# Loading the FFN weights by casting DMAs, V straight into its padded tile, and the first two batches by head pairs, in a fused ReLU²-attention and SwiGLU kernel

## The chip, the cores and the metric

The kernel runs on one core of one Trainium2 chip. The metric is device time in microseconds (us) of one execution. The engines are called PE (TensorE, matmuls), PEld (its weight loads), DVE (VectorE), ACT (ScalarE), POOL (GpSimd) and SP (SyncE, which here only issues DMAs).

## The reference

```python
def _attn_ref(q, k, v):                      # each (8, 12, 448, 64), float32
    scores = (1 / sqrt(64)) * (q @ k.T)
    attn = np.maximum(scores, 0.0) ** 2 / 448
    return attn @ v

def _moe_ref(x, w_gate, w_val, w_out, rms_g):   # x: (3584, 768)
    xn = x / sqrt(mean(x * x) + 1e-6) * rms_g
    g = xn @ w_gate                          # (768, 1536)
    val = xn @ w_val                         # (768, 1536)
    return (g * sigmoid(g) * val) @ w_out    # (1536, 768)

# x is the attention's output, (8, 12, 448, 64) -> (8*448, 12*64)
```

Each of the three weight matrices has 768 x 1536 float32 values, 4.72 MB. The output is float32.

## The kernel before

The kernel computes in bf16. It handles one batch of attention as six head pairs (2 x 64 = 128 partitions). While it computes the attention of batch b it inserts the FFN of batch b-1 in chunks ("fillers") between and inside the pairs. Batch 0 has no FFN to insert. There the fillers are 60 pieces of weight loading, ten per pair: a float32 piece comes by a DMA on SP's queue into one of four staging tiles, and ScalarE casts it into the bf16 weight tile.

```python
wstage = ctx.enter_context(tc.tile_pool(name="wstage", bufs=4))
ldpool = ctx.enter_context(tc.tile_pool(name="ld", bufs=2))
apool  = ctx.enter_context(tc.tile_pool(name="attn", bufs=10))
# ... cut ...
def _wload(src_d, dst_sb, kt, o, w):                 # 60 of these: wwork
    st = wstage.tile([P, WCH], FP32, name="wst", tag="wst")
    nc.sync.dma_start(out=st[:, :w], in_=src_d[:, kt, o : o + w])
    nc.scalar.copy(out=dst_sb[:, kt, o : o + w], in_=st[:, :w])
# ... cut ...
def load_batch(b):
    if b == 0:      # per pair and per tensor: tiles qp, kp, vp by casting GpSimd DMAs
        ...
    # other batches: one casting GpSimd DMA each for q, k and v: tiles qb, kb, vb
# ... cut ...
def attention_pair(b, j, xT, qkv, fillers=()):
    # PE transposes q and k into psT; ScalarE copies them to QT and KT
    # ... cut ...
    vpad = ldpool.tile([PC, NCH, 2, P], BF16, name="vpad", tag="vpad")
    nc.vector.tensor_copy(out=vpad[:, :, 0, 0:D], in_=vb[:, :, 0, :])
    nc.vector.tensor_copy(out=vpad[:, :, 0, D:P], in_=zero_bf[:PC])
    nc.vector.tensor_copy(out=vpad[:, :, 1, 0:D], in_=zero_bf[:PC])
    nc.vector.tensor_copy(out=vpad[:, :, 1, D:P], in_=vb[:, :, 1, :])
    for c in range(NCH):
        # PE: psS = K Q^T for both heads; ScalarE: ReLU of the first (rA);
        # VectorE: ReLU of the second (rB), and both squares
        ...
    if fillers: fillers.pop(0)()
    # PE: psAV += vpad^T rA / rB, eight matmuls
    if fillers: fillers.pop(0)()
    nc.scalar.mul(out=xT[:, j, :], in_=psAV[:], mul=inv_attn)
    for f in fillers: f()
# ... cut ...
# main loop: the fillers are the FFN chunks of batch b-1, and wwork for b == 0
```

A scheduler fixes the order of instructions on each engine when the kernel is built.

Of the kernel before, what the change touches and what calls it, by code (L numbers as in the profile page):

```python
# [9 lines left out]
FP32 = mybir.dt.float32  # L10
BF16 = mybir.dt.bfloat16
# [7 lines left out]
def kernel(  # L19
# [11 lines left out]
    nc = tc.nc  # L31
    P = nc.NUM_PARTITIONS

    B, H, S, D = q.shape
    T, DM = out.shape
    DMw, F = moe_w_gate.shape
# [3 lines left out]
    NCH = 4  # L40
    assert S % NCH == 0
    PC = S // NCH
    assert PC <= P
    assert DM % P == 0 and F % P == 0
    KT = DM // P
    FT = F // P
    HP = H // 2
# [12 lines left out]

    const_pool = ctx.enter_context(tc.tile_pool(name="consts", bufs=1))
    wpool = ctx.enter_context(tc.tile_pool(name="weights", bufs=1))
    wstage = ctx.enter_context(tc.tile_pool(name="wstage", bufs=4))
    ldpool = ctx.enter_context(tc.tile_pool(name="ld", bufs=2))
    tpool = ctx.enter_context(tc.tile_pool(name="tsb", bufs=2))
    apool = ctx.enter_context(tc.tile_pool(name="attn", bufs=10))
    xpool = ctx.enter_context(tc.tile_pool(name="xT", bufs=2))
    npool = ctx.enter_context(tc.tile_pool(name="norm", bufs=2))
    hpool = ctx.enter_context(tc.tile_pool(name="hT", bufs=2))
# [18 lines left out]
    zero_bf = const_pool.tile([P, NCH, D], BF16, name="zero_bf", tag="zero_bf")  # L88
# [2 lines left out]
    g_sb = wpool.tile([P, KT], FP32, name="g_sb", tag="rmsg")  # L91
    nc.sync.dma_start(out=g_sb[:], in_=moe_rms_g.rearrange("(kt p) -> p kt", p=P))

    wg_sb = wpool.tile([P, KT, F], BF16, name="wg_sb", tag="wg")
    wv_sb = wpool.tile([P, KT, F], BF16, name="wv_sb", tag="wv")
    wo_sb = wpool.tile([P, FT, DM], BF16, name="wo_sb", tag="wo")
    wg_d = moe_w_gate.rearrange("(kt p) f -> p kt f", p=P)
    wv_d = moe_w_val.rearrange("(kt p) f -> p kt f", p=P)
    wo_d = moe_w_out.rearrange("(fk p) m -> p fk m", p=P)
    WCH = 512  # L100
    wwork: list = []

    def _wload(src_d, dst_sb, kt, o, w):
        st = wstage.tile([P, WCH], FP32, name="wst", tag="wst")
        nc.sync.dma_start(out=st[:, :w], in_=src_d[:, kt, o : o + w])
        nc.scalar.copy(out=dst_sb[:, kt, o : o + w], in_=st[:, :w])

    for src_d, dst_sb, nk in ((wg_d, wg_sb, KT), (wv_d, wv_sb, KT), (wo_d, wo_sb, FT)):
        W = dst_sb.shape[-1]
        for kt in range(nk):  # L110
            for o in range(0, W, WCH):
                w = min(WCH, W - o)
                wwork.append(
                    lambda a=(src_d, dst_sb, kt, o, w): _wload(*a)
                )

    def qkv_batch_ap(t: bass.AP, b: int) -> bass.AP:
        return t[b].rearrange("h (p c) d -> p c h d", c=NCH)

    def qkv_pair_ap(t: bass.AP, b: int, j: int) -> bass.AP:  # L120
        return t[b, 2 * j : 2 * j + 2].rearrange("h (p c) d -> p c h d", c=NCH)

    def out_rows_ap(b: int) -> bass.AP:
        return out[b * S : (b + 1) * S, :].rearrange("(p u) m -> p u m", u=NCH)

    def load_batch(b: int):
        if b == 0:
            out_tiles = []
            for j in range(HP):
                trip = []  # L130
                for src, tg in ((q, "qp"), (k, "kp"), (v, "vp")):
                    t = ldpool.tile([PC, NCH, 2, D], BF16, name=tg, tag=tg)
                    nc.gpsimd.dma_start(out=t[:], in_=qkv_pair_ap(src, b, j))
                    trip.append(t[:])
                out_tiles.append(tuple(trip))
            return out_tiles
        big = []
        for src, tg in ((q, "qb"), (k, "kb"), (v, "vb")):
            t = ldpool.tile([PC, NCH, H, D], BF16, name=tg, tag=tg)
            nc.gpsimd.dma_start(out=t[:], in_=qkv_batch_ap(src, b))  # L140
            big.append(t)
        return [
            tuple(t[:, :, 2 * j : 2 * j + 2, :] for t in big) for j in range(HP)
        ]

    def attention_pair(b: int, j: int, xT: bass.AP, qkv, fillers=()):
        fillers = list(fillers)
        qb, kb, vb = qkv
        QT = tpool.tile([P, S], BF16, name="QT", tag="QT")
        KT_ = tpool.tile([P, S], BF16, name="KT", tag="KT")  # L150
        psT = psum.tile([P, 2, S], BF16, name="psT", tag="psS", bufs=PSS_BUFS)
        for ti, (src, dst) in enumerate(((qb, QT), (kb, KT_))):
            for c in range(NCH):
                nc.tensor.transpose(  # L154
                    out=psT[:, ti, c * PC : (c + 1) * PC],
                    in_=src[:, c, :, :],
                    identity=ident[:],
                )
            nc.scalar.copy(out=dst[:], in_=psT[:, ti, :])  # L159

        vpad = ldpool.tile([PC, NCH, 2, P], BF16, name="vpad", tag="vpad")
        nc.vector.tensor_copy(out=vpad[:, :, 0, 0:D], in_=vb[:, :, 0, :])
        nc.vector.tensor_copy(out=vpad[:, :, 0, D:P], in_=zero_bf[:PC])
        nc.vector.tensor_copy(out=vpad[:, :, 1, 0:D], in_=zero_bf[:PC])
        nc.vector.tensor_copy(out=vpad[:, :, 1, D:P], in_=vb[:, :, 1, :])  # L165

        psAV = psum.tile([P, S], FP32, name="psAV", tag="psAV", bufs=1)
        rsq = [[None] * NCH, [None] * NCH]
        for c in range(NCH):
            pss = []  # L170
            for hh in range(2):
                prt = slice(hh * D, (hh + 1) * D)
                if b == 0:
                    tg, bf = _ps0_tags[(j * NCH * 2 + c * 2 + hh) % len(_ps0_tags)]
                else:
                    tg, bf = "psS", PSS_BUFS
                psS = psum.tile([PC, S], FP32, name="psS", tag=tg, bufs=bf)
                nc.tensor.matmul(  # L178
                    out=psS[:],
                    lhsT=KT_[prt, c * PC : (c + 1) * PC],  # L180
                    rhs=QT[prt, :],
                    start=True,
                    stop=True,
                )
                pss.append(psS)
            rA = apool.tile([PC, S], BF16, name="rA", tag="rA")
            nc.scalar.activation(out=rA[:], in_=pss[0][:], func=ACT.Relu)  # L187
            nc.vector.tensor_tensor(out=rA[:], in0=rA[:], in1=rA[:], op=ALU.mult)  # L188
            rsq[0][c] = rA
            rB = apool.tile([PC, S], BF16, name="rB", tag="rA")  # L190
            nc.vector.tensor_relu(out=rB[:], in_=pss[1][:])  # L191
            nc.vector.tensor_tensor(out=rB[:], in0=rB[:], in1=rB[:], op=ALU.mult)  # L192
            rsq[1][c] = rB
        if fillers:
            fillers.pop(0)()
        for hh in range(2):
            for c in range(NCH):
                nc.tensor.matmul(  # L198
                    out=psAV[:],
                    lhsT=vpad[:, c, hh, :],  # L200
                    rhs=rsq[hh][c][:],
                    start=(hh == 0 and c == 0),
                    stop=(hh == 1 and c == NCH - 1),
                )
        if fillers:
            fillers.pop(0)()
        nc.scalar.mul(out=xT[:, j, :], in_=psAV[:], mul=inv_attn)  # L207
        for f in fillers:
            f()
# [98 lines left out]
    for b in range(NB):  # L308
        xT = xpool.tile([P, KT, S], BF16, name="xT", tag="xT")
        xTs.append(xT)  # L310
        qkvs = load_batch(b)
        if b >= 1:
            work = ffn_chunks(b - 1, xTs[b - 1])
        else:
            work = wwork
        per = (len(work) + HP - 1) // HP
        wi = 0
        for j in range(HP):
            fl = work[wi : wi + per]
            wi += len(fl)  # L320
            attention_pair(b, j, xT, qkvs[j], fillers=fl)
        while wi < len(work):
            work[wi]()
            wi += 1
# [31 lines left out]
```

## Time and profile before

The median is 678.0 us (675.4 to 682.0, 16 runs). Three times of the profiled execution (span 677.0 us):

| what | time |
|---|---|
| first gate matmul (psG), where the FFN of batch 0 begins | 104.6 us |
| PE busy before it, and after it | 51.0 of 104.6 us; 537.7 of 572.4 us |
| time between the normalisations of successive batches later on (taken at their square root, tile rstdb) | 75.1 to 75.7 us |

The first fence is from the page: busy time of each engine, then three rows of the span in 40 slices of 17 us (a digit is the busy share in tenths; PEclk is the granted clock in tenths).

```profile
PE 588.8 (87%) x3120; PEld 296.7 (44%) x3120; DVE 463.2 (68%) x1088; ACT 272.5 (40%) x517; POOL 69.8 (10%) x48
PE   0655469999899989999899979999899989997997
PEclk9999999999699988999699989999799989999899
DMA  9999940069100890069001890079000110001002
```

PE is the limit from the seventh slice on. The first six slices, about 104 us, are different: PE is half idle while the DMA engines are busy. The clock row reads 9 there, but the matmuls themselves say otherwise. A score matmul (psS) took 577 ns (median, 20 to 40 us) and 393 ns later, from 180 to 220 us. The Trainium skill, "TensorE: Matmul & The Clock Gate", Part 1, says that an idle PE gets half its clock and gets the full clock after about 3.4 us of sustained work. The trace agrees with the half: near 181 us, where the clock row dips, successive gate and value matmuls start 0.37 us apart, and 0.19 us apart at 190 us. Before 108.4 us the clock column must not be read: the trace has no clock record there, its first record is a change to full speed, and the views count time without a record as full speed.

The second fence is the table of waits of the window 0 to 104 us. The columns are who waited for whom, then us in total, number of waits, longest one.

```profile
PE psT L154 <- ACT QT L159: 20.1, 7, 9.8
ACT wv_sb L106 <- DMA wst<-in_moe_w_val_dram: 14.8, 14, 2.4
ACT wg_sb L106 <- DMA wst<-in_moe_w_gate_dram: 12.9, 11, 2.7
ACT wo_sb L106 <- DMA wst<-in_moe_w_out_dram: 12.6, 12, 1.9
```

ScalarE waited 40 us (14.8 + 12.9 + 12.6) for staged weights, and PE waited 20 us for ScalarE's copy of a transposed q. The third fence, from the timeline (start, us, engine, line, instruction, count, idle time before it and what ended that):

```profile
18.19 0.62 ACT L106 CAST wg_sb<-wst 128x512 bf16<-128x512 f32 x1 [1.51 <-DMA wst<-in_moe_w_gate_dram]
18.72 0.53 ACT L159 COPY QT<-psT 128x448 bf16<-128x448 bf16 x1
19.30 0.53 PE L154 MATMUL psT<-ident,kp 112*128 112x112 bf16 x4 [9.79 <-ACT QT L159]
```

The first q had landed at 8.95 us, where its transposes start. The copy that takes them out of PSUM (the memory that PE writes to) ran at 18.72, because it stands behind casts in ScalarE's fixed order, and each cast waits for its own load. PE stood for 9.79 us. The skill's "TensorE: Matmul & The Clock Gate", Part 1, in the passage on engine queue depths, calls ScalarE's queue strictly first in, first out.

The last fence is from the view of DMA queues for 0 to 100 us (queue, kind, packets, MB, share of the 16 engines' time).

```profile
q0 software_dynamic: 48768, 6.19, 96.9%
q1 hardware_dynamic: 9424, 14.16, 49.5%
```

The staged weights (q1) moved 14.16 MB in about 100 us, while GpSimd's queue (q0: batches 0, 1 and 2 of q, k and v) held the same engines with many small packets. The packets of the two queues overlap in time, so the shares add up to more than 100%.

### The profile page before, as it was taken

Reading aid. Unit: us, or ns where it says so; the run is one execution under the profiler, and the core shown is the slowest. Engines: PE = TensorE matmul, PEld = TensorE weight load, DVE = VectorE, ACT = ScalarE, POOL = GpSimd, SP = SyncE. Lnnn points to the kernel's source line nnn. Section 1 sums busy time; section 2 is a strip of 40 time slices with the busy share of each in tenths; the row PEclk is TensorE's granted clock in tenths of the full one; section 3 lists DMA queues with packets and bytes.
Section 4 is the critical chain, followed back from the end, with each engine's and each line's share of the span. In section 5 each row is a group of like instructions: output and inputs, shape, how many; then the busy total and the mean of one; then the engine's idle time right before and its main releaser. Section 6 shows DMA issues by size and latency. Waiting matters only on the chain. (4 is left out here: it accounts for less than half of the span.)

```text
span 677.0 us, 8435 instructions
## 1 busy us (share of the span) xinstructions
PE 588.8 (87%) x3120; PEld 296.7 (44%) x3120; DVE 463.2 (68%) x1088; ACT 272.5 (40%) x517; POOL 69.8 (10%) x48
## 2 busy tenths in 40 slices
PE   0655469999899989999899979999899989997997
PEld 0212124456244544456344644455344634454455
DVE  0533369786888679775888678866978578857552
ACT  3755573532544243532534243433434253422210
POOL 5653000012001200012001200012000000000000
PEclk9999999999699988999699989999799989999899
DMA  9999940069100890069001890079000110001002
GB/s 197 219 233 225 207 125 1 1 41 135 30 0 4 89 113 1 1 41 145 20 0 12 89 105 1 1 62 143 1 1 1 42 42 0 1 21 61 1 1 81
DMA packets 143208, 42.22 MB, mean 62 GB/s; under 512 B 131904, under 2 KB 133440, under 8 KB 143168
## 3 DMA queue, kind: packets, MB, share of 16 engines
q0 software_dynamic: 129648, 16.52, 38.2%
q1 hardware_dynamic: 13520, 25.17, 12.5%
q8 instruction: 24, 0.39, 0.2%
q14 instruction: 16, 0.13, 0.1%
HBM read 47.19 MB, written 11.01 MB: 86 GB/s over the span
## 5 line engine op out<-in xcount | busy, mean ns | idle before, releaser
L256 PE MATMUL psG<-xn,wg_sb 128*128 128x448 bf16 x576 | 152.0, 365 | 6.8 <-DVE xn L238 4.4
L191 DVE TENSOR_SCALAR rB<-psS 112x448 bf16<-112x448 f32 x192 | 116.8, 616 | 45.2 <-PE psS L178 45.2
L265 PE MATMUL psV<-xn,wv_sb 128*128 128x448 bf16 x576 | 140.5, 360 | 0.2 <-DVE hT L276 0.2
L289 PE MATMUL psO<-wo_sb,hT 128*112 128x512 bf16 (+1 forms) x768 | 136.2, 327 | 0.0
L178 PE MATMUL psS<-QT,KT 64*112 64x448 bf16 x384 | 92.4, 428 | 32.7 <-ACT rA L187 14.5
L289 PEld LDWEIGHTS <-hT 128*112 128x112 bf16 x768 | 90.4, 130 | 38.5 <-issue 7.0
L187 ACT ACTIVATE rA<-psS 112x448 bf16<-112x448 f32 x192 | 97.7, 541 | 18.5 <-PE psS L178 17.8
L273 ACT ACTIVATE sig<-psG 128x448 bf16<-128x448 f32 x96 | 51.4, 543 | 115.5 <-PE psG L256 77.8
L188 DVE TENSOR_TENSOR rA<-rA 112x448 bf16<-112x448 bf16 x192 | 73.3, 382 | 23.8 <-ACT rA L187 23.3
L265 PEld LDWEIGHTS <-wv_sb 128*128 128x128 bf16 x576 | 54.7, 99 | 65.3 <-issue 22.7
L256 PEld LDWEIGHTS <-wg_sb 128*128 128x128 bf16 x576 | 55.3, 100 | 61.6 <-issue 23.5
L275 DVE TENSOR_TENSOR t<-sig,psG 128x448 bf16<-128x448 bf16 x96 | 58.6, 616 | 33.2 <-ACT sig L273 31.9
L198 PE MATMUL psAV<-rA,vpad 112*128 112x448 bf16 x192 | 66.7, 405 | 10.6 <-DVE rA L188 9.6
L192 DVE TENSOR_TENSOR rB<-rB 112x448 bf16<-112x448 bf16 x192 | 73.4, 382 | 0.1
L276 DVE TENSOR_TENSOR hT<-t,psV 128x448 bf16<-128x448 bf16 x96 | 59.3, 618 | 17.4 <-PE psV L265 13.7
L296 DVE COPY ost<-psO 112x512 f32<-112x512 f32 x64 | 35.5, 555 | 48.0 <-PE psO L289 48.0
L178 PEld LDWEIGHTS <-KT 64*112 64x112 bf16 x384 | 29.8, 140 | 87.2 <-issue 56.6
L207 ACT ACTIVATE xT<-psAV 128x448 bf16<-128x448 f32 x48 | 26.2, 546 | 98.6 <-PE psAV L198 98.6
L198 PEld LDWEIGHTS <-vpad 112*128 112x128 bf16 x384 | 38.2, 107 | 57.7 <-issue 33.8
L198 PE MATMUL psAV<-rB,vpad 112*128 112x448 bf16 x192 | 59.4, 414 | 0.0
L159 ACT COPY QT<-psT 128x448 bf16<-128x448 bf16 x48 | 25.4, 530 | 79.4 <-PE psT L154 79.4
L140 POOL DMA_DIRECT2D vb<-in_v_dram x7 | 16.6, 2372 | 290.3 <-DVE vpad L165 290.3
(41 smaller groups left out, 344.5 us busy)
## 6 DMA issues: line engine op xcount, KB each, us to landing
out_dram<-ost SPq DMA_DIRECT2D x32, 336.0 KB, 2.7
qb<-in_q_dram POOLq DMA_DIRECT2D x7, 672.0 KB, 9.3
kb<-in_k_dram POOLq DMA_DIRECT2D x7, 672.0 KB, 12.5
vb<-in_v_dram POOLq DMA_DIRECT2D x7, 672.0 KB, 8.9
wst<-in_moe_w_gate_dram SPq DMA_DIRECT2D x18, 256.0 KB, 5.0
wst<-in_moe_w_val_dram SPq DMA_DIRECT2D x18, 256.0 KB, 6.5
wst<-in_moe_w_out_dram SPq DMA_DIRECT2D x12, 256.0 KB, 6.5
wst<-in_moe_w_out_dram SPq DMA_DIRECT2D x12, 128.0 KB, 6.1
```

Of the source, the lines that this page charges most:

```text
L178: nc.tensor.matmul(out=psS[:], lhsT=KT_[prt, c * PC : (c + 1) * PC], rhs=QT[prt, :], start=True, stop=True,)
L187: nc.scalar.activation(out=rA[:], in_=pss[0][:], func=ACT.Relu)
L188: nc.vector.tensor_tensor(out=rA[:], in0=rA[:], in1=rA[:], op=ALU.mult)
L191: nc.vector.tensor_relu(out=rB[:], in_=pss[1][:])
L192: nc.vector.tensor_tensor(out=rB[:], in0=rB[:], in1=rB[:], op=ALU.mult)
L198: nc.tensor.matmul(out=psAV[:], lhsT=vpad[:, c, hh, :], rhs=rsq[hh][c][:], start=(hh == 0 and c == 0), stop=(hh == 1 and c == NCH - 1),)
L256: nc.tensor.matmul(out=psG[:], lhsT=wg_sb[:, kt, fb * P : (fb + 1) * P], rhs=xn[:, kt, :], start=(kt == 0), stop=(kt == KT - 1),)
L265: nc.tensor.matmul(out=psV[:], lhsT=wv_sb[:, kt, fb * P : (fb + 1) * P], rhs=xn[:, kt, :], start=(kt == 0), stop=(kt == KT - 1),)
L273: nc.scalar.activation(out=sig[:], in_=psG[:], func=ACT.Sigmoid)
L275: nc.vector.tensor_tensor(out=t1[:], in0=sig[:], in1=psG[:], op=ALU.mult)
L276: nc.vector.tensor_tensor(out=hT[:, fb, :], in0=t1[:], in1=psV[:], op=ALU.mult)
L289: nc.tensor.matmul(out=psO[:, :w], lhsT=hT[:, fk, u * PC : (u + 1) * PC], rhs=wo_sb[:, fk, o : o + w], start=(fk == 0), stop=(fk == FT - 1),)
```

## The change

The intent is to take the weight staging off SP and ScalarE, to take the V copies off VectorE, and to have everything that start-up needs requested early:

1. Each weight matrix comes by one GpSimd DMA that casts float32 to bf16 on the way. The staging pool, 60 loads and 60 casts go.
2. V comes by two GpSimd DMAs per pair straight into the padded tile. Of four VectorE copies per pair the two zero fills remain, given to any engine.
3. Batches 0 and 1 are loaded by pairs, with six buffers per tile in place of two. The order of requests is batch 0, wg, wv, batch 1's pairs 0 to 2, wo, batch 1's pairs 3 to 5.
4. The pool for rA and rB grows from 10 to 20 buffers.

```diff
-    wstage = ctx.enter_context(tc.tile_pool(name="wstage", bufs=4))
-    apool = ctx.enter_context(tc.tile_pool(name="attn", bufs=10))
+    apool = ctx.enter_context(tc.tile_pool(name="attn", bufs=20))
... cut ...
+    def load_vpad(b: int, j: int):
+        vpad = ldpool.tile([PC, NCH, 2, P], BF16, name="vpad", tag="vpad", bufs=6)
+        nc.any.tensor_copy(out=vpad[:, :, 0, D:P], in_=zero_bf[:PC])
+        nc.any.tensor_copy(out=vpad[:, :, 1, 0:D], in_=zero_bf[:PC])
+        nc.gpsimd.dma_start(out=vpad[:, :, 0, 0:D], in_=v_head_ap(b, 2 * j))
+        nc.gpsimd.dma_start(out=vpad[:, :, 1, D:P], in_=v_head_ap(b, 2 * j + 1))
+        return vpad
... cut: load_batch(b, pairs): q and k by pairs with bufs=6 for batches 0 and 1, whole
... batches later; V always by load_vpad; the result for batch 1 is kept in `early` ...
-    def _wload(src_d, dst_sb, kt, o, w):
-        st = wstage.tile([P, WCH], FP32, name="wst", tag="wst")
-        nc.sync.dma_start(out=st[:, :w], in_=src_d[:, kt, o : o + w])
-        nc.scalar.copy(out=dst_sb[:, kt, o : o + w], in_=st[:, :w])
... cut ...
+    def load_weights():
+        nc.gpsimd.dma_start(out=wg_sb[:], in_=moe_w_gate.rearrange("(kt p) f -> p kt f", p=P))
+        nc.gpsimd.dma_start(out=wv_sb[:], in_=moe_w_val.rearrange("(kt p) f -> p kt f", p=P))
+        first = load_batch(1, range(0, 3))
+        nc.gpsimd.dma_start(out=wo_sb[:], in_=moe_w_out.rearrange("(fk p) m -> p fk m", p=P))
+        early[1] = first + load_batch(1, range(3, HP))
... cut: the four vpad copies leave attention_pair ...
         qkvs = load_batch(b)
-        if b >= 1:
+        if b == 0:
+            load_weights()
+            work = []
+        else:
             work = ffn_chunks(b - 1, xTs[b - 1])
-        else:
-            work = wwork
```

More of the change, by code (lines that the diff above doesn't have):

```diff
@@ L92, with qk_batch_ap, qk_pair_ap, v_head_ap @@
     nc.sync.dma_start(out=g_sb[:], in_=moe_rms_g.rearrange("(kt p) -> p kt", p=P))
+    def qk_batch_ap(t: bass.AP, b: int) -> bass.AP:
+        return t[b].rearrange("h (p c) d -> p c h d", c=NCH)
+    def qk_pair_ap(t: bass.AP, b: int, j: int) -> bass.AP:
+        return t[b, 2 * j : 2 * j + 2].rearrange("h (p c) d -> p c h d", c=NCH)
+    def v_head_ap(b: int, h: int) -> bass.AP:
+        return v[b, h].rearrange("(p c) d -> p c d", c=NCH)
+    def out_rows_ap(b: int) -> bass.AP:
+        return out[b * S : (b + 1) * S, :].rearrange("(p u) m -> p u m", u=NCH)
+    def load_vpad(b: int, j: int):
[5 more added lines that the diff above has]
+        return vpad
+    early: dict = {}
+    def load_batch(b: int, pairs=None):
+        if b in early:
+            return early[b]
+        if b == 0 or pairs is not None:
+            trips = []
+            for j in pairs if pairs is not None else range(HP):
+                qkp = []
+                for src, tg in ((q, "qp"), (k, "kp")):
+                    t = ldpool.tile([PC, NCH, 2, D], BF16, name=tg, tag=tg, bufs=6)
+                    nc.gpsimd.dma_start(out=t[:], in_=qk_pair_ap(src, b, j))
+                    qkp.append(t[:])
+                trips.append((qkp[0], qkp[1], load_vpad(b, j)))
+            return trips
+        big = []
+        for src, tg in ((q, "qb"), (k, "kb")):
+            t = ldpool.tile([PC, NCH, H, D], BF16, name=tg, tag=tg)
+            nc.gpsimd.dma_start(out=t[:], in_=qk_batch_ap(src, b))
+            big.append(t)
+        return [
+            (
+                big[0][:, :, 2 * j : 2 * j + 2, :],
+                big[1][:, :, 2 * j : 2 * j + 2, :],
+                load_vpad(b, j),
+            )
+            for j in range(HP)
+        ]
     wg_sb = wpool.tile([P, KT, F], BF16, name="wg_sb", tag="wg")
@@ L96 @@
     wo_sb = wpool.tile([P, FT, DM], BF16, name="wo_sb", tag="wo")
-    wg_d = moe_w_gate.rearrange("(kt p) f -> p kt f", p=P)
-    wv_d = moe_w_val.rearrange("(kt p) f -> p kt f", p=P)
-    wo_d = moe_w_out.rearrange("(fk p) m -> p fk m", p=P)
-    WCH = 512
-    wwork: list = []
-    def _wload(src_d, dst_sb, kt, o, w):
-        st = wstage.tile([P, WCH], FP32, name="wst", tag="wst")
-        nc.sync.dma_start(out=st[:, :w], in_=src_d[:, kt, o : o + w])
-        nc.scalar.copy(out=dst_sb[:, kt, o : o + w], in_=st[:, :w])
@@ L108 @@
-    for src_d, dst_sb, nk in ((wg_d, wg_sb, KT), (wv_d, wv_sb, KT), (wo_d, wo_sb, FT)):
-        W = dst_sb.shape[-1]
-        for kt in range(nk):
-            for o in range(0, W, WCH):
-                w = min(WCH, W - o)
-                wwork.append(
-                    lambda a=(src_d, dst_sb, kt, o, w): _wload(*a)
-                )
-    def qkv_batch_ap(t: bass.AP, b: int) -> bass.AP:
-        return t[b].rearrange("h (p c) d -> p c h d", c=NCH)
-    def qkv_pair_ap(t: bass.AP, b: int, j: int) -> bass.AP:
-        return t[b, 2 * j : 2 * j + 2].rearrange("h (p c) d -> p c h d", c=NCH)
@@ L123, in out_rows_ap @@
-    def out_rows_ap(b: int) -> bass.AP:
-        return out[b * S : (b + 1) * S, :].rearrange("(p u) m -> p u m", u=NCH)
-    def load_batch(b: int):
-        if b == 0:
-            out_tiles = []
-            for j in range(HP):
-                trip = []
-                for src, tg in ((q, "qp"), (k, "kp"), (v, "vp")):
-                    t = ldpool.tile([PC, NCH, 2, D], BF16, name=tg, tag=tg)
-                    nc.gpsimd.dma_start(out=t[:], in_=qkv_pair_ap(src, b, j))
-                    trip.append(t[:])
-                out_tiles.append(tuple(trip))
-            return out_tiles
-        big = []
-        for src, tg in ((q, "qb"), (k, "kb"), (v, "vb")):
-            t = ldpool.tile([PC, NCH, H, D], BF16, name=tg, tag=tg)
-            nc.gpsimd.dma_start(out=t[:], in_=qkv_batch_ap(src, b))
-            big.append(t)
-        return [
-            tuple(t[:, :, 2 * j : 2 * j + 2, :] for t in big) for j in range(HP)
-        ]
+    def load_weights():
+        nc.gpsimd.dma_start(
+            out=wg_sb[:], in_=moe_w_gate.rearrange("(kt p) f -> p kt f", p=P)
+        )
+        nc.gpsimd.dma_start(
+            out=wv_sb[:], in_=moe_w_val.rearrange("(kt p) f -> p kt f", p=P)
+        )
+        first = load_batch(1, range(0, 3))
+        nc.gpsimd.dma_start(
+            out=wo_sb[:], in_=moe_w_out.rearrange("(fk p) m -> p fk m", p=P)
+        )
+        early[1] = first + load_batch(1, range(3, HP))
@@ L146, in attention_pair @@
     def attention_pair(b: int, j: int, xT: bass.AP, qkv, fillers=()):
         fillers = list(fillers)
-        qb, kb, vb = qkv
+        qb, kb, vpad = qkv
         QT = tpool.tile([P, S], BF16, name="QT", tag="QT")
@@ L159, in attention_pair @@
             nc.scalar.copy(out=dst[:], in_=psT[:, ti, :])
-        vpad = ldpool.tile([PC, NCH, 2, P], BF16, name="vpad", tag="vpad")
-        nc.vector.tensor_copy(out=vpad[:, :, 0, 0:D], in_=vb[:, :, 0, :])
-        nc.vector.tensor_copy(out=vpad[:, :, 0, D:P], in_=zero_bf[:PC])
-        nc.vector.tensor_copy(out=vpad[:, :, 1, 0:D], in_=zero_bf[:PC])
-        nc.vector.tensor_copy(out=vpad[:, :, 1, D:P], in_=vb[:, :, 1, :])
         psAV = psum.tile([P, S], FP32, name="psAV", tag="psAV", bufs=1)
```

## The prediction

> **What bounds the kernel now.** Two stages.
> (a) Start-up, 0 to about 104 us. By the tile view of wg_sb the first gate matmul runs at 104.6 us. The windows view gives PE 46.7 us of 100 busy up to there, while DMA moves 157 to 232 GB/s until 95 us: batch 0's and 1's q, k, v, batch 2's and all weights (14.2 MB as float32) share the engines. The timeline shows batch 0's pairs starved: first q issued at 1.6 us, landed at 8.95; loads have two buffers, so GpSimd issues later ones only when slots come free; a pair takes about 10 us. ScalarE's 60 weight casts (0.62 or 0.40 us) wait for staging loads and sit between the copies and ReLUs that PE needs. Matmuls here take 0.53-0.59 us: slow clock.
> (b) From 104 us on PE is the limit: 28 matmuls per 5 us, PE busy 95-100%, period 75.1-75.7 us per batch (GpSimd's q issues at 156.6, 232.3, 308.0, 383.7, 458.8). Exception: at each batch boundary the normalisation leaves about 4 us of PE gaps, and the granted clock falls to 0.50-0.65 for some 10 us. The Trainium skill, "TensorE: Matmul & The Clock Gate", Part 1, says an idle PE drops to half rate until it has been busy for about 3.4 us; the trace agrees (0.58 us at 180 us, 0.19 us later).
>
> **What the change does.** Removes 192 VectorE V/zero copies (0.14 us apart, 27 us of VectorE in all), leaving 96 zero copies for whichever engine; removes 60 ScalarE casts (about 33 us) and the staging loads. V lands in the padded tile by 96 GpSimd DMAs instead of 13; weights come by three casting DMAs. Batch 0 gets six buffers, so all its loads go first, then wg, wv, batch 1 pairs 0-2, wo, pairs 3-5. The built order shows the same PE order at later boundaries; at the first one, batch 1's third pair is transposed before the first gate instead of after it.
>
> **Cost.** VectorE and ScalarE are not the limit in (b): the removals are worth 0 to 4 us there. The gain is (a). Steady q/k/v transfers go at about 106 GB/s (0.69 MB in 6.5 us), so a batch takes about 20 us. Weights: the same bytes per matrix (4.7 MB) at the 297 GB/s of engine time (hardware queue: 25.2 MB, 12.5% of the span) give 16 us, an estimate; if the cast ran at the q/k/v element rate, 22 us. The skill's "DMA: Bandwidth & Descriptors" (SWDGE vs HWDGE) says that casts need GpSimd's queue and that all queues share 16 engines, so bytes read do not shrink. Batch 0 by about 23 us, wg 39, wv 55, batch 1's first three pairs 65 (pessimistic 80). In parallel, eight pairs of attention at 6-7 us (VectorE 5.5, slow PE 7) end near 60 us. First gate: about 67 us, 37 us earlier. wo (81 us) and pairs 3-5 (91 us) come just in time, for use at about 110 and 87 us. Everything after shifts by the same amount.
>
> **Predicted** 642 us, range 630 to 658. Faster by over 2%: 0.94; within 2%: 0.05; slower: 0.01.
>
> **What shows each step.** First gate at 60-80 us; psO first at 100-125 us; period still 75 us with the clock dips; POOL issues all 24 batch-0 DMAs within about 20 us; ACT busy down by 30 us, DVE by 30; wg's landing 14-22 us after its turn; last batches unchanged.
>
> **What would make it wrong.** Casting DMAs of long rows slower than the q/k/v element rate, so that the first gate comes at 90 us or later; PE, in fixed order, held by batch 1's later pairs behind wo, leaving holes and slow clock in the first FFN stage; GpSimd descriptor writing held up; or the boundary gaps closing (then faster than 630).

## The result, and the profile after

The changed kernel is correct and takes 642.6 us (641.4 to 643.8, 10 runs) against 678.0. The ratio is 0.9475, with a 95% interval of 0.9458 to 0.9491. Ratios here are the mean time of one kernel's fast runs over that of the other's of the same rounds, so they are not quite the ratio of the medians.

The page after has these lines in place of those shown of before:

```profile
PE 582.0 (91%) x3120; PEld 293.9 (46%) x3120; DVE 449.3 (70%) x965; ACT 251.5 (39%) x484; POOL 124.5 (19%) x144
PE   5956899979999899989999899997999889997997
PEclk9995899989999699997999889997999979998999
DMA  9999997222119511391124912197113300011002
wg_sb<-in_moe_w_gate_dram POOLq DMA_DIRECT2D x1, 2304.0 KB, 19.3
wv_sb<-in_moe_w_val_dram POOLq DMA_DIRECT2D x1, 2304.0 KB, 28.9
wo_sb<-in_moe_w_out_dram POOLq DMA_DIRECT2D x1, 2304.0 KB, 15.5
```

The start-up is four slices of 16 us in place of six of 17. From there on the PE row looks like before's. The last three lines are DMA issues (KB written, us from issue to landing). wg was issued at 20.1 us, wv at 21.6 and wo at 54.7, so they landed at 39.4, 50.5 and 70.2 us. wv landed 11.1 us after wg.

The tile view of wg_sb gives the first gate matmul (durations in ns: least, median, most; then first and last start), first for the kernel before:

```profile
L256 PE MATMUL psG<-xn,wg_sb x576: 349/352/578, 104.6 to 655.4; 128*128 128x448 bf16 x192
```

and for the kernel after:

```profile
L264 PE MATMUL psG<-xn,wg_sb x576: 349/352/581, 71.7 to 618.8; 128*128 128x448 bf16 x192
```

The gate starts 32.9 us earlier (104.6 to 71.7), and the span is 36.6 us shorter (677.0 to 640.4). So 90% of the gain is had before the first FFN matmul. Of the other 3.7 us, 1.8 come between the first gate and the normalisation of batch 1 (66.6 us before, 64.8 after); the normalisations of batches 0 and 1 stand 73.6 us apart before and 69.3 after. The next five distances add up to 377.3 us before and 375.3 after (each 75.1 or 75.7 before, 74.8 or 75.4 after), which gives another 2.0. No run explains these 2 us; a second profile of the changed kernel (after_again) has 375.9.

The view by windows shows the start-up (window; length; busy us and instructions of PE, PEld, DVE, ACT and POOL; clock; DMA share; GB/s). Before:

```profile
0.00:20.00 20.00, 1.08 (x8) 0.71 (x8) 0.99 (x6) 7.93 (x13) 9.20 (x16) 1.00 1.20 199
40.00:60.00 20.00, 10.78 (x33) 3.54 (x33) 10.62 (x32) 10.99 (x23) 7.57 (x5) 1.00 1.83 232
80.00:100.00 20.00, 11.26 (x36) 3.69 (x36) 11.00 (x28) 14.31 (x30) 0.00 (x0) 1.00 0.78 157
```

After:

```profile
0.00:20.00 20.00, 11.89 (x53) 4.72 (x53) 12.33 (x34) 9.85 (x19) 19.43 (x33) 1.00 1.24 78
40.00:60.00 20.00, 9.60 (x40) 3.68 (x40) 10.09 (x25) 6.03 (x14) 9.80 (x13) 0.62 1.40 159
80.00:100.00 20.00, 19.77 (x110) 9.53 (x107) 14.15 (x30) 8.49 (x18) 7.85 (x8) 1.00 2.47 128
```

PE runs 53 matmuls and transposes in the first 20 us in place of 8, and by 80 us it is full. The table of waits of after (0 to 104 us) puts PE's wait for the copy of q at 2.2 us, in place of 20.1. PE's longest waits are now for q itself:

```profile
PE psT L168 <- ACT QT L173: 2.2, 5, 0.7
PE psT L168 <- DMA qp<-in_q_dram: 13.5, 2, 8.2
```

One window of after is still poor: from 40 to 60 us PE works 9.60 us. The timeline of the kernel after shows why:

```profile
21.63 3.25 POOL L150 DMA_DIRECT2D wv_sb<-in_moe_w_val_dram  x1
22.45 3.60 POOL L124 DMA_DIRECT2D qp<-in_q_dram  x1
...
39.95 0.72 POOL L109 DMA_DIRECT2D vpad<-in_v_dram  x1 [9.17 <-DMA wg_sb<-in_moe_w_gate_dram]
50.85 0.70 POOL L110 DMA_DIRECT2D vpad<-in_v_dram  x1 [10.18 <-DMA wv_sb<-in_moe_w_val_dram]
51.33 0.55 PE L168 MATMUL psT<-ident,qp 112*128 112x112 bf16 x4 [8.19 <-DMA qp<-in_q_dram]
```

The seventh q to be requested, that of batch 1's first pair, was issued at 22.45 us, just behind wv, and PE got it at 51.33, just after wv had landed (50.5). PE's order has the transposes of this pair ahead of the last matmuls of batch 0's attention, so PE had nothing to do from 43.1 to 51.3 us, and batch 0's normalisation began only at 61.1. PE's speed does not set this: in after_again the clock was up from 11.3 us on (31.2 in after, by the first clock records of the two traces), PE was busy for 1.3 of the ten us from 40 to 50 (2.4 in after), and the first gate came at 70.9. The two GpSimd lines are another matter: one issue waited until wg had landed, and the next until wv had. Each is the eighth DMA after the one that it waits for, and so is the next that waited, at 70.46 us for wo. That looks like a set of eight completion semaphores used in turn, but this is inferred from the count; no run tested it. It did not make the hole, since the q was issued long before, but it held back the requests for batch 1's third pair until 51.57 us.

### The profile page after: what moved, and what is told of

The parts are those of the page before. It is cut to its first block, busy times and chain, and to the rows that moved or that the text cites. A ratio compares the mean times of both kernels' runs of the same rounds, so it can differ in the third digit from the quotient of the medians.

```text
span 640.4 us, 8306 instructions
## 1 busy us (share of the span) xinstructions
PE 582.0 (91%) x3120; PEld 293.9 (46%) x3120; DVE 449.3 (70%) x965; ACT 251.5 (39%) x484; POOL 124.5 (19%) x144
## 4 chain that ended last, share of the span: by engine, by line
PE 70%; DVE 13%; ACT 7%; DMA 5%; POOL 3%; issue 2%; ACTq 0%; POOLq 0%
PE psO L297 20%; PE psV L273 16%; PE psG L264 15%; PE psAV L206 9%; PE psS L186 7%; DMA qp<-in_q_dram 5%; DVE xn L246 4%; DVE rstdb L243 3%; ACT rA L195 3%; PE psT L168 3%; DVE rB L199 2%; DVE rB L200 2%; DVE rA L196 1%; POOL qp L124 1%; POOL kp L124 1%
## 5 line engine op out<-in xcount | busy, mean ns | idle before, releaser
L109 POOL DMA_DIRECT2D vpad<-in_v_dram x48 | 53.3, 1126 | 337.6 <-PE psAV L206 175.4
L273 PEld LDWEIGHTS <-wv_sb 128*128 128x128 bf16 x576 | 54.6, 99 | 66.6 <-issue 22.8
L196 DVE TENSOR_TENSOR rA<-rA 112x448 bf16<-112x448 bf16 x192 | 73.3, 382 | 16.2 <-ACT rA L195 15.8
L264 PEld LDWEIGHTS <-wg_sb 128*128 128x128 bf16 x576 | 55.5, 100 | 60.0 <-issue 21.6
L206 PE MATMUL psAV<-rA,vpad 112*128 112x448 bf16 x192 | 63.3, 391 | 1.9 <-DVE rA L196 0.6
L206 PEld LDWEIGHTS <-vpad 112*128 112x128 bf16 x384 | 36.9, 104 | 49.4 <-issue 28.5
```

Of the source, the lines that this page charges most:

```text
L109: nc.gpsimd.dma_start(out=vpad[:, :, 0, 0:D], in_=v_head_ap(b, 2 * j))
L196: nc.vector.tensor_tensor(out=rA[:], in0=rA[:], in1=rA[:], op=ALU.mult)
L206: nc.tensor.matmul(out=psAV[:], lhsT=vpad[:, c, hh, :], rhs=rsq[hh][c][:], start=(hh == 0 and c == 0), stop=(hh == 1 and c == NCH - 1),)
L264: nc.tensor.matmul(out=psG[:], lhsT=wg_sb[:, kt, fb * P : (fb + 1) * P], rhs=xn[:, kt, :], start=(kt == 0), stop=(kt == KT - 1),)
L273: nc.tensor.matmul(out=psV[:], lhsT=wv_sb[:, kt, fb * P : (fb + 1) * P], rhs=xn[:, kt, :], start=(kt == 0), stop=(kt == KT - 1),)
```

## The experiments

Four explanations of the 36 us were open after the result:

- The weight path: staged weights stand in ScalarE's order and hold batch 0's attention; casting DMAs take them out of it.
- The loads: batch 0's and 1's q, k and v come earlier, through more buffers.
- The busy time taken from ScalarE (casts) or VectorE (copies).
- The larger pool for rA and rB.

Each kernel was compared with the kernel before on the same chip. In the table, "rest" is the profiled span less the time of the first gate matmul. It tells start-up from all the work after it. These two columns are of the profiled run, which for weights_first (674.2 us) and b1_first9 (639.3) is the slowest of its four.

| kernel | median us | ratio to before [95%] | first gate | rest |
|---|---|---|---|---|
| before | 678.0 | 1 | 104.6 | 572.4 |
| after | 642.6 | 0.9475 [0.9458, 0.9491] | 71.7 | 568.7 |
| weights_only | 648.6 | 0.9571 [0.9519, 0.9623] | 64.0 | 580.4 |
| loads_only | 679.7 | 1.0022 [0.9975, 1.0069] | 106.7 | 571.6 |
| act_back | 642.5 | 0.9464 [0.9411, 0.9517] | 70.3 | 570.5 |
| dve_back | 660.2 | 0.9736 [0.9691, 0.9781] | 73.3 | 585.0 |
| two_bufs | 649.2 | 0.9595 [0.9572, 0.9618] | 74.2 | 572.2 |
| weights_first | 669.5 | 0.9905 [0.9861, 0.9950] | 101.8 | 570.4 |
| b1_first9 | 635.7 | 0.9389 [0.9336, 0.9441] | 66.9 | 570.4 |
| attn10 | 641.7 | 0.9491 [0.9458, 0.9525] | 71.3 | 568.0 |
| casts_late | 669.5 | 0.9892 [0.9850, 0.9934] | 91.3 | 574.5 |
| dve_back2 | 674.4 | 0.9973 [0.9940, 1.0006] | 73.6 | 598.1 |
| b1_first9_again | 633.5 | 0.9356 [0.9322, 0.9390] | 59.0 | 568.8 |
| after_again | 642.0 | 0.9480 [0.9450, 0.9510] | 70.9 | 570.1 |

All gave correct results.

### weights_only: the kernel before with nothing but the three casting DMAs

```diff
-    wstage = ctx.enter_context(tc.tile_pool(name="wstage", bufs=4))
... staging loads and casts removed ...
+    def load_weights():
+        nc.gpsimd.dma_start(out=wg_sb[:], in_=wg_d)
+        nc.gpsimd.dma_start(out=wv_sb[:], in_=wv_d)
+        nc.gpsimd.dma_start(out=wo_sb[:], in_=wo_d)
... in the main loop, after load_batch(0) ...
-            work = wwork
+            load_weights()
+            work = []
```

> The kernel before with one part of the change: the three casting DMAs replace the staged weight loads and the 60 ScalarE casts; q, k, v loads, their two buffers and the VectorE padding stay. Theory (start-up supply: the order and earliness of what the FFN needs): about half of the gain, first gate at 75 to 90 us, 650 to 662 us. Rival A (it is the ScalarE casts alone): nearly the whole gain, 640 to 648. Rival B (it is the VectorE padding alone): no gain, 672 to 682.

It took 648.6 us, a little better than the expected range and 0.6 us above rival A's, so the number alone does not tell the two apart; act_back and loads_only do. By the ratios, this one part gives 29 us (4.3% of 678.0) where the whole change gives 36 (5.25%). The first gate comes at 64.0 us, earlier than expected (75 to 90) and even earlier than in after, but the rest is 580.4 us, 8 more than before's. The normalisations of batches 0 and 1 stand 80.8 us apart (73.6 before), because batch 1's q and k are requested behind all three weights, as the timeline shows:

```profile
63.55 0.56 PE L143 MATMUL psT<-ident,qb 112*128 112x112 bf16 x4 [5.29 <-DMA qb<-in_q_dram]
68.16 0.56 PE L143 MATMUL psT<-ident,kb 112*128 112x112 bf16 x4 [0.99 <-DMA kb<-in_k_dram]
```

So the weight path is the main part. What this version lacks lies in the stage of these two waits (6.3 us together); no run mended the order of batch 1's loads alone.

### loads_only: everything but the weight path

```diff
     # the changed kernel, with the staging pool, _wload and wwork of before put back
+    wstage = ctx.enter_context(tc.tile_pool(name="wstage", bufs=4))
     def load_weights():
-        ... three casting DMAs, batch 1 in two parts ...
+        early[1] = load_batch(1, range(0, HP))
...
-            work = []
+            work = wwork
```

> The changed kernel with the weights loaded as before (staged on the hardware queue, cast by ScalarE), all the rest of the change kept: batches 0 and 1 by pairs with six buffers, V straight into the padded tile. Theory: weights and batch 0 share the DMA engines again and the casts stand in ScalarE's line, so only part of the gain: first gate at 82 to 98 us, 655 to 668 us. Rival A (ScalarE casts alone): no gain, 675 to 680. Rival B (VectorE padding alone): whole gain, 640 to 646.

It took 679.7 us: no gain at all, a miss, and the number that was expected of rival A. Early loads, six buffers, fewer VectorE copies and the larger pool together are worth nothing while the staged weights and their casts stay. The waits of its window 0 to 104 us name the same pair as before:

```profile
PE psT L179 <- ACT QT L184: 21.8, 6, 10.2
ACT wo_sb L156 <- DMA wst<-in_moe_w_out_dram: 17.0, 15, 2.7
ACT wg_sb L156 <- DMA wst<-in_moe_w_gate_dram: 16.0, 13, 2.5
```

ScalarE's waits for staging come to 41 us (16.0 + 17.0, and 8.0 for wv); they were 40 before. The first QT copy stands at 18.63 us (18.72 before), although more of batch 0 had been requested by then. By the trace, all 24 loads of batch 0 had landed by 33.1 us (25.8 in after), and yet its normalisation began at 91.4. So late q, k and v are not what held the attention; the block is in ScalarE's order. Why the staged pieces came so slowly is not separated: they shared the DMA engines with q, k and v, and they had only four buffers. The casts of wv started 1.8 us apart on average in before, and 0.8 in casts_late (below), where little else was under way and there were 16 buffers.

### act_back: ScalarE's work put back, without its waits

```diff
             load_weights()
-            work = []
+            cin = wpool.tile([P, 512], FP32, name="cin", tag="cin")
+            nc.vector.memset(cin[:], 0.0)
+            def cast(wd):
+                cd = tpool.tile([P, 512], BF16, name="cd", tag="cd", bufs=4)
+                nc.scalar.copy(out=cd[:, :wd], in_=cin[:, :wd])
+            work = [lambda wd=wd: cast(wd) for wd in [512] * 36 + [512, 256] * 12]
```

> The changed kernel with 60 ScalarE casts of a zeroed scratch tile put back as fillers of batch 0 (36 of 512 columns, 12 of 512 and 12 of 256), which depend on no DMA; results unchanged. Theory: ScalarE is half idle in the start-up and the DMAs set its length, so 0 to 8 us are lost (642 to 650). Rival A (the gain is ScalarE's relief): 25 to 35 us are lost (667 to 678).

It took 642.5 us, as after. Sixty casts of the same sizes at the same places in batch 0, reading a tile that is ready, cost nothing that can be seen in the time. So what hurt before was mainly not the time of the casts but what they waited for. The casts did delay the attention, though: the first score matmul came at 12.8 us (7.9 in after). From 40 to 50 us, where after has its hole, PE was busy; first act_back, then after:

```profile
40.00:50.00 10.00, 8.35 (x32) 3.47 (x30) 5.76 (x17) 8.77 (x22) 0.25 (x1) 1.00 1.33 201
40.00:50.00 10.00, 2.42 (x12) 0.73 (x11) 5.10 (x14) 2.20 (x5) 0.67 (x1) 0.74 1.34 201
```

The casts used up the wait for batch 1's q. Up to the 8 us of that wait could therefore show in a kernel without it; no run put the casts into b1_first9. This run also rules out the clock as the source of the gain: its first clock record stands at 72.5 us, so PE was slow through the whole start-up (577 ns for a score matmul), and the first gate came at 70.3 all the same.

### casts_late: staged weights, but the casts behind batch 0's attention

This version takes loads_only, gives it 16 staging buffers (and 10 buffers for rA and rB, for room), and puts all casts after batch 0's last pair. A one-column VectorE write from xT into each weight block keeps the scheduler from moving them forward; the casts overwrite it.

```diff
-    wstage = ... bufs=4
+    wstage = ... bufs=16
-            work = wwork
+            work = []
...
+        if b == 0:
+            for wsb, nk, st in ((wg_sb, KT, 512), (wv_sb, KT, 512), (wo_sb, FT, 512)):
+                for o in range((wsb.shape[-1] + st - 1) // st):
+                    nc.vector.tensor_copy(
+                        out=wsb[:, :, o * st : o * st + 1],
+                        in_=xT[:, HP - 1, 0:nk].rearrange("p (k o) -> p k o", o=1))
+            for f in wwork:
+                f()
```

> loads_only (staged weights on the hardware queue, cast by ScalarE, everything else as changed) with the 60 casts held back until batch 0's attention is done: a tiny VectorE write of the last pair's result into each weight tile comes before its cast. Staging has 16 buffers instead of 4 and the attention pool 10. Theory after loads_only and act_back: what cost 36 us was neither ScalarE's time nor the shared DMA engines, but batch 0's copies and ReLUs standing in ScalarE's fixed order behind casts whose staging loads had not landed. Then attention of batch 0 ends near 45 us, 36 casts and the rest of the weight loads follow, first gate at 65 to 80 us, 640 to 655 us. Rival (the hardware-queue path and the sharing of the DMA engines are slow in themselves): first gate at 90 us or later, 665 to 680 us.

It took 669.5 us, a miss: this time and the first gate, 91.3 us, are what was expected of the rival. The trace splits it. What was to be freed was freed: batch 0's attention ended near 60 us (not near 45, as expected), and its normalisation began at 62.0 us (91.6 before, 61.1 after). But the first 16 of the 60 pieces filled the buffers, and the next load was issued at 61.33 us, when the casts had begun. The windows show the price:

```profile
60.00:66.00 6.00, 4.61 (x14) 1.53 (x13) 4.37 (x15) 5.59 (x12) 2.96 (x2) 0.50 2.55 156
66.00:87.00 21.00, 1.79 (x5) 0.71 (x5) 0.69 (x2) 17.55 (x31) 2.27 (x1) 0.50 1.24 321
```

For 21 us PE does almost nothing while the last of wg and all of wv are cast (wv's last cast starts at 83.7 us). The waits of 55 to 95 us show the same block as in before, now in batch 1:

```profile
DVE rA L207 <- ACT rA L206: 20.8, 2, 20.4
PE psAV L217 <- DVE rA L207: 19.2, 1, 19.2
ACT wv_sb L156 <- DMA wst<-in_moe_w_val_dram: 3.4, 14, 0.3
```

The ReLU that both wait for ran at 84.20 us, behind those casts. ScalarE itself waited only 3.4 us for pieces of wv, so here the casts' own work is most of the price, and a slow queue, the rival, the smaller part. Staged weights either hold the attention (before) or come after it (here). The casting DMA escapes both, since it needs no ScalarE and no staging buffers. The skill's "DMA: Bandwidth & Descriptors", section "SWDGE vs HWDGE vs iDMA", says that a cast in a DMA can only be issued from GpSimd; every casting DMA is issued there, and no run tried another queue.

### two_bufs: the changed kernel with two buffers per tile again

```diff
-   ... name=tg, tag=tg, bufs=6)
+   ... name=tg, tag=tg, bufs=2)
-   ... name="vpad", tag="vpad", bufs=6)
+   ... name="vpad", tag="vpad", bufs=2)
```

> The changed kernel with two buffers instead of six for the pair tiles of q, k and the padded V. Loads wait for slots again and stand in line with the weights on GpSimd's queue. Theory: a good part of the gain goes, first gate at 80 to 95 us, 650 to 665 us; and V loads come only two pairs ahead in the later batches, which costs 0 to 5 us more. If buffers do not matter: 641 to 645.

It took 649.2 us: 7 us more than after, a smaller effect than expected. The first gate is 2.5 us later and the first output matmul (psO) 3.6 us later (116.0 against 112.4). The buffers are worth something only once the weight path is mended; in loads_only they gave nothing.

### weights_first: the same transfers in another order

```diff
-        qkvs = load_batch(b)
         if b == 0:
             load_weights()           # now only wg, wv, wo
             work = []
+        qkvs = load_batch(b)
+        if b == 0:
+            early[1] = load_batch(1, range(HP))
```

> The changed kernel with the three weight DMAs issued ahead of batch 0's pairs; batch 1's pairs after batch 0's. Same bytes, same engines' work, other order. The trace of the changed kernel shows wg and wv landing 11.1 us apart, so the weights take about 34 us in which attention has nothing to do; then batches 0 and half of 1 follow with 35 us. Theory (order of supply counts): first gate at 85 to 100 us, 660 to 675 us. Rivals (relief of an engine, or the faster weight path as such): order is worth little, 640 to 648.

It took 669.5 us, as expected. The same DMAs with the three weights ahead of batch 0 lose 27 us of the 36: the attention starves instead, and the first gate comes at 101.8 us, just later than expected. Being cheap does not make the casting DMA a gain by itself; it must also stand behind what is needed first.

### attn10: the pool for rA and rB at 10 again

```diff
-    apool = ctx.enter_context(tc.tile_pool(name="attn", bufs=20))
+    apool = ctx.enter_context(tc.tile_pool(name="attn", bufs=10))
```

> The changed kernel with the attention pool back at 10 buffers. The built order up to the first gate is the same. Theory: not part of the gain, 641 to 645 us. If the deeper pool lets attention run ahead: 646 or more.

It took 641.7 us. The larger pool has no part in the gain.

### dve_back and dve_back2: VectorE's copies put back

```diff
+        vdum = ldpool.tile([PC, NCH, 2, P], BF16, name="vdum", tag="vdum")
+        nc.vector.tensor_copy(out=vdum[:, :, 0, 0:D], in_=kb[:, :, 0, :])
+        nc.vector.tensor_copy(out=vdum[:, :, 0, D:P], in_=zero_bf[:PC])
+        nc.vector.tensor_copy(out=vdum[:, :, 1, 0:D], in_=zero_bf[:PC])
+        nc.vector.tensor_copy(out=vdum[:, :, 1, D:P], in_=kb[:, :, 1, :])
```

> The changed kernel with four VectorE copies of 112x256 per head pair into a scratch tile nobody reads, as many as the padding took before; results unchanged. Theory: PE is the limit outside the start-up, so 0 to 5 us are lost (642 to 648). Rival B (the gain is VectorE's relief): 20 to 30 us are lost (662 to 672).

It took 660.2 us, 18 more than after: a miss, just short of rival B's range. The copies read the loaded k, and the scheduler put the next batch's copies early in VectorE's order. The table of waits of the whole run shows VectorE waiting for a load that it had never waited for:

```profile
DVE vdum L176 <- DMA kb<-in_k_dram: 14.8, 5, 3.8
```

At 214.96 us, for example, VectorE starts after 3.4 us of such a wait and then runs 24 of the copies, those of six pairs, before the ReLU that PE needs; PE is busy for 1.0 of the 5 us from 214.7. The experiment had brought in a wait and a bunching of its own, so it was repeated with copies that read QT, which is ready when the pair is:

```diff
+        vdum = ldpool.tile([PC, NCH, 2, P], BF16, name="vdum", tag="vdum")
+        qtv = QT[:PC, 0 : NCH * D].rearrange("p (c d) -> p c d", c=NCH)
+        for hh2 in range(2):
+            for o2 in (0, D):
+                nc.vector.tensor_copy(out=vdum[:, :, hh2, o2 : o2 + D], in_=qtv)
```

> dve_back again, without its flaw: there the scratch copies read the next batch's K, were placed early in VectorE's fixed order, and VectorE waited 14.8 us in five waits for K to land. Here the four copies per pair read the pair's own transposed Q. Theory (VectorE has room outside the start-up): 642 to 648 us. If VectorE's relief itself is worth something: 655 or more, as dve_back had.

It took 674.4 us, again a miss, and a larger one, on the side that was to speak for VectorE's relief. The timeline of dve_back2 has the reason at the point where each batch's next q and k are requested:

```profile
200.36 2.29 POOL L131 DMA_DIRECT2D qb<-in_q_dram  x1 [5.54 <-PE psT L168]
200.66 4.41 DVE L179 COPY vdum<-QT 112x256 bf16<-112x256 bf16 x4 [0.34 <-ACT QT L173]
202.35 2.60 POOL L131 DMA_DIRECT2D kb<-in_k_dram  x1
205.65 0.40 PE L192 MATMUL psS<-QT,KT 64*112 64x448 bf16 x2 [2.62 <-DVE rB L205]
```

Four copies take 4.41 us in all; the tile view gives a median of 0.221 us for one, and 2.315 at most. They coincide with GpSimd's two issues, here and at 282 us. PE then waits 2.62 us for VectorE, and the granted clock falls (0.66 from 205 to 210 us). The time between normalisations rises to 81.0 to 81.8 us from 75 in the four stages that hold such a pair of issues (200, 282, 362 and 444 us). In the next stage, which has the copies but no such issues, it is 76.4. The skill's "SBUF — State Buffer", section "SBUF: two separate sides", describes an exclusive lock between a GpSimd operation and a VectorE operation in a two-port mode: whichever starts first has the port pair for the whole instruction, and the other blocks. The coincidence agrees with that. So the trace ties the loss to GpSimd's issues, but no run took these away alone, and the lock itself isn't shown.

These two runs do not price the copies that the change removed. They show that 192 copies are not free wherever they are put. The real ones are in weights_only, which keeps all 192: its five distances from the normalisation of batch 1 to that of batch 6 add up to 375.6 us, against 375.3 in after. In those stages they cost nothing that can be seen. What they cost in start-up is not separated: weights_only is 6 us slower than after in all, with an earlier gate and later loads of batch 1 among the reasons.

### b1_first9: batch 1's first three pairs ahead of the weights

The hole at 43 to 51 us led to this one, which requests batch 1's pairs 0 to 2 before wg. It has nine buffers, so that they fit beside batch 0's six; order and buffers are thus tested together.

```diff
     def load_weights():
+        first = load_batch(1, range(0, 3))
         nc.gpsimd.dma_start(out=wg_sb[:], ...)
         nc.gpsimd.dma_start(out=wv_sb[:], ...)
-        first = load_batch(1, range(0, 3))
...
-   bufs=6     (qp, kp and vpad)
+   bufs=9
```

> The changed kernel with batch 1's first three pairs loaded ahead of wg and wv, and nine buffers for the pair tiles so that they need not wait for slots. The trace of the changed kernel shows GpSimd's issue of batch 1's second V held until wg and then wv had landed (39.9 and 50.8 us), and PE without work from 43.1 to 51.3 us and at half clock until about 66. Theory: that hole goes, attention runs on to its eighth pair by about 55 us, wg and wv land by about 58, first gate at 57 to 64 us, 628 to 636 us: faster than both kernels. If the 71.7 us of the first gate are set by PE or ScalarE work rather than by this hole: 640 to 645.

It took 635.7 us, faster than after, but its four runs lie between 630.6 and 639.3, and the profiled one is the slowest of them, with its first gate at 66.9 us in place of the expected 57 to 64. The hole is gone (PE is busy 18.08 us of 40 to 60). In that profile PE was slow instead: score matmuls took 616 ns (median) from 20 to 60 us. So it was run again, beside after.

> Repeat of b1_first9 beside the changed kernel on the same chip, to see whether it beats it. Its first runs were 630.6 to 639.3 us (first gate at 66.9 us in the profile, PE at half clock all through the start-up). Theory: 632 to 638 us, 0.985 to 0.995 of the changed kernel's time.

> The changed kernel itself, unaltered, as the partner of b1_first9_again on the same chip: 641 to 645 us.

The second time it took 633.5 us (629.8 to 635.7) and after took 642.0 (640.6 to 642.8), on the same chip. Relative to after that is 0.9356 / 0.9480 = 0.987. In this profile the first gate is at 59.0 us, batch 0's normalisation begins at 48.5 us (61.1 in after, 57.3 in the first profile of b1_first9), and the score matmuls took 393 ns from 8 to 36 us: the clock was up for the first half of the start-up. The tile view of psS from 20 to 40 us in the first profile:

```profile
L186 PE MATMUL psS<-QT,KT x24: 574/616/621, 21.2 to 38.7; 64*112 64x448 bf16 x24
```

and of the same window in the second:

```profile
L186 PE MATMUL psS<-QT,KT x25: 349/393/621, 19.7 to 36.5; 64*112 64x448 bf16 x25
```

The same program got another clock in start-up: the first clock record, a change to full speed, stands at 62.0 us in the first trace and at 11.7 us in the second. The skill's Part 1 on the clock gate says that the window which measures activity runs freely, so that the moment of the warm-up varies by about half a microsecond between runs. A change from run to run agrees, but 50 us is not that size, and two profiles cannot show the cause. Of all the kernels run, this is the fastest.

## Why the prediction was right or wrong

The total, 642 predicted and 642.6 measured, is right, and so is the main claim: the gain is in start-up, and from the second FFN stage on hardly anything changes (2 us). The same sum was reached with some terms off in opposite directions, so that it came out to within 1 us is partly luck.

- **The shift.** First gate predicted at about 67 us, measured 71.7; psO first at 100 to 125, measured 112.4. Right in range. The prediction took a shift of 37 us; it was 32.9, and 3.7 more came after the first gate, inside the 0 to 4 us allowed for the rest.
- **Requests and landings.** All 24 loads of batch 0 were to be issued in about 20 us; they were issued from 1.6 to 19.4. wg by 39 (39.4) is right by two errors that cancel: batch 0 was to have landed by 23 us and took until 25.8, and wg then took 13.6 us in place of 16. wv by 55 was pessimistic (50.5): 16 us per matrix was the estimate, 11.1 us was measured. The estimate came from the staged queue's rate in engine time. The skill's "DMA: Bandwidth & Descriptors", section "Anatomy of one DMA", gives a fit of 2.0 us plus bytes over 436,000 per us; on the 4.72 MB read that is an estimate of 12.8 us, closer.
- **The term that ate this.** Cheaper weights should have brought the gate forward. They did not, because of the 8 us hole at 43 to 51 us. The step that failed is "in parallel, eight pairs of attention at 6-7 us ... end near 60 us". It supposed an unbroken run, although the prediction's own list of landings had batch 1's first pair behind wv. Six pairs took until about 43 us, and the seventh had to wait for its q. b1_first9 puts these loads first. It is 6 us faster than attn10, the nearest to after in its round, in the first trial, and 8.5 us faster than after in the second.
- **Why start-up was slow before.** The prediction gave three reasons: two buffers, shared DMA engines, and casts that "sit between the copies and ReLUs". It gave them no weights. The runs do. The casts' waits in ScalarE's order are the one that matters: taking away the staged loads with their casts gains 29 us (weights_only); doing all the rest and leaving them gains nothing (loads_only). How far the shared engines made those waits long is not separated. The buffers are worth 7 us once the casts are gone (two_bufs), and nothing before.
- **Engine relief.** ScalarE was to be down by 30 us and fell by 21.0 (272.5 to 251.5): 60 casts went, but 27 of the 96 zero fills went to it, at 0.405 us each. VectorE was to be down by 30 and fell by 13.9 (463.2 to 449.3): the other 69 fills stayed there, and some took up to 1.55 us, where no padding copy took more than 0.32 us before. ScalarE's part cost no time in this kernel (act_back), where the wait for batch 1's q could hide up to 8 us of it. VectorE's part was argued as 0 to 4 us; outside the start-up no more than 0.3 us of it shows (weights_only against after), and in start-up it remains unmeasured.
- **Steady state.** The time between normalisations, 75 us predicted, is 74.8 or 75.4 (75.1 or 75.7 before), and the clock still dips at each batch boundary: 0.50 from 215 to 220 us, as from 175 to 180 before. Right.

Four things stay open: the worth of the removed V copies in start-up; why the staged pieces came slowly before, shared engines or four buffers; whether a set of eight completion semaphores is what holds GpSimd's issues; and whether the port lock is what stretches VectorE's copies.

## What to carry to other kernels

An engine that works in order passes its waits on to everything behind it, so price a cast by what it waits for and not by its 0.6 us: 60 casts with data ready cost nothing here (their delay fell into another wait), and with 60 casts waiting for staged loads batch 0's normalisation began 30 us later. When several large transfers feed the start, put the requests in the order of use, and ask which request each idle stretch was waiting for; here that order was worth 27 us (weights_first) and another 8.5 (b1_first9_again). When you add work to an engine in order to test its cost, check in the trace that the work has not brought a wait of its own.

## What the Trainium skill lacked or had wrong

- "DMA: Bandwidth & Descriptors" says that casts need GpSimd's queue but has no rate for a casting DMA. Here a 768 x 1536 matrix, 4.72 MB of float32 read and 2.36 MB of bf16 written, landed 11.1 us after the one before it (wg at 39.4, wv at 50.5). That is 425 GB/s of what is read, an estimate from these two times. The same distance is 11.0 to 11.1 us in the traces of act_back, attn10, after_again, weights_first and both of b1_first9.
- The same page, under "Issuing engine by pattern", calls the hardware queues generally faster. These runs do not show it for the weights, nor do they compare like with like: with little else under way, all DMAs together, mainly the staged 256 KB loads, moved 321 GB/s (casts_late, 66 to 87 us), against the 425 above, but ScalarE had to empty the staging buffers and was busy for 17.55 of those 21 us.
- No page that I read tells of a GpSimd issue that waits for the landing of the eighth DMA before it. Such waits of 9.2, 10.2 and 7.8 us stand in the trace of after. Whether hardware or the built program makes them is not settled.
- "SBUF — State Buffer" tells of VectorE holding up GpSimd's descriptors, and says that the loser of the lock blocks, whichever it is. For the reverse case it has only a bare ratio (VectorE 6.8 times slower), without the operations. Here, beside GpSimd issues of 2.3 and 2.6 us, copies of 0.22 us took up to 2.3 us, and PE lost 2.6 us.
- "TensorE: Matmul & The Clock Gate" warns that the clock events of a trace have been seen to be unreliable, but not that they may only begin with the first change to full speed. In before the first record stands at 108.4 us, so the clock column read 1.00 from 20 to 40 us, while score matmuls took 577 ns in place of 393. The same page has the warm-up vary by 0.5 us between runs; here the first record of one program stood at 11.7 and at 62.0 us.
